# A scan, an ELU layer and a gated layer in one kernel: three reorderings in the first block

## The chip, the cores and the metric

The kernel runs on one core of a Trainium2 chip. The metric is the device time of one execution, in microseconds (us); of several runs the median counts. The engines are TensorE (PE, its weight loads apart as PEld), VectorE (DVE), ScalarE (ACT), GpSimd (POOL) and the transfer queue of SyncE (SP), which issues every DMA.

## The reference

Three steps follow each other on 3072 tokens: a chunked scan over 4 batches of 768 positions and 8 heads, and two feed-forward layers on its output.

```python
# per chunk: la = log(clip(a)), cum = cumsum(la)
L = exp(cum[i] - cum[j]) * causal
y = (C @ B.T * L) @ x + (C @ state) * exp(cum)
state = exp(sum(la)) * state + sum_j(B x exp(cum[-1] - cum[j]))
# x = y as (3072 tokens, 256)
h = x @ w_in                                   # 256 -> 2048
g = where(h > 0, h, exp(min(h, 0)) - 1)
x = g @ w_out                                  # 2048 -> 256
g = x @ w_gate; val = x @ w_val                # 256 -> 1536
out = (g * sigmoid(g) * val) @ w_out2          # 1536 -> 256
```

All weights come as 64-bit floats and must first be turned into 32-bit ones; matmuls are done in pieces of a high and a low part, to keep the accuracy.

## The kernel before

The 3072 tokens are cut into six blocks of 512. A **slot** is one pair of a block and a tile of 128 hidden units: sixteen slots a block in the first layer (96 in all), then twelve a block in the gated layer (72). The main loop runs over slots, and in each it writes out, in this order: the matmuls h of the slot (`m_a`, L489), the tasks listed under `early`, the first evacuation of h on ACT (L511), the exponential (L516) and the maximum on DVE (L517), the second matmuls c of an earlier slot (two slots back in block 0, `m_c`, L531), and then the tasks listed under `mid` and under `late`. The order written out is the order of each engine's queue: nothing reorders it later.

The scan is cut into 24 **units** of 128 tokens. Units 0 to 3, needed for block 0, come first by a hand-written list (`ORDER`). The units of block b+1 run inside the slots of block b, four of them: units 4 to 7 in block 0, at slots 0, 3, 6 and 9 (`FIRST`). From unit 8 on a unit begins every four slots, three slots earlier than a block's own count would have it (`BASE`), so unit 8 begins in slot 13 of block 0. `OFF` and `OFF1` say for each stage of a unit in which slot after its first one it stands, and in which list ("e", "m" and "l" for early, mid and late). Units from 8 on (`CUT`) have another form: their scores cb (`pe1`, L366) need operands zb and zc, split in a high part on ACT (`hi`, L294) and a low part, zb's on POOL and zc's on DVE (`lo`, L300). A unit's loads (`a_load`: abc L250 or L255, bcraw L241 or L243, ahn) are asked two units ahead. The stages that matter below are u (L388, matmuls into the accumulators y), y (L447, L454), out (xh, L470, ACT reads y) and xl (L474, DVE reads y). From unit 4 on all units share one set of accumulators.

In block 0 the weights of the first layer are still being made ready, tile by tile (f = 0 to 15; the first three ahead of the slots). Tile f takes these steps:

- `load_w1(f)`: SP asks for 512 KB into one of five areas of the buffer w2e, in turn by f modulo 5 (L127).
- `ex_w1(f)`: ACT makes e from the words with the exponents (L133). e has a single buffer.
- `dec_w1(f)`: three steps on DVE, d0 (L136) and d1 (L139) from the raw words and d2 (L143), which needs e, make the 32-bit value v.
- `pair_w1(f)`: ACT rounds v to the high part w1h (L175), and POOL subtracts, which gives the low part w1l (L179).

In slot s the kernel makes e of tile s+4 and loads tile s+7; it decodes tile s+3 and makes its pair.

Of the kernel before, what the change touches and what calls it, by code (L numbers as in the profile page):

```python
# [22 lines left out]
CUT = 8  # L23
# [15 lines left out]
OFF = dict(hi=(-1, "l"), lo=(0, "m"), scan=(0, "l"), pe1=(1, "l"), mid=(2, "m"), u=(2, "l"), state=(3, "e"), pe2=(4, "l"), out=(4, "l"), xl=(4, "l"))  # L39

OFF1 = dict(OFF, hi=(-2, "l"), lo=(-1, "m"), pe1=(0, "l"), u=(4, "l"), state=(5, "e"))
W2S = 16
FIRST = [0,3,6,9]
RAWB = 2
# [3 lines left out]
LEAD = 4  # L48
# [18 lines left out]
def ssm_mlp_glu_kernel(ctx, tc, a, bcs, xbc, w1, w2, consts, out):  # L67
# [117 lines left out]
    spare, at = {}, [0, 0]  # L185
# [450 lines left out]
    with tc.manual_schedule():  # L636
# [3 lines left out]
        nw = NW  # L640
# [25 lines left out]
        early, mid, pe, late = {}, {}, {}, {}  # L666
        late[8] = [(lambda: nc.scalar.activation(ident8, ident.unsqueeze(1).to_broadcast([128, H, Q]), AF.Copy), ())]

        def at(when, slot, fn, *args):
            when.setdefault(slot, []).append((fn, args))  # L670

        t = n0
        for b in range(NB - 1):
            n_u = BLOCKS[b + 1] // Q
            step = NF1 // n_u
            for k in range(n_u):
                s0 = b * NF1 + (FIRST[k] if b == 0 else k * step + BASE)
                off, order = (OFF, list(STAGES)) if t < CUT else (OFF1, "hi lo scan pe1 mid pe2 u out xl state".split())
                for st in order:
                    fn, (o, w) = STAGES[st], off[st]  # L680
                    at(dict(e=early, m=mid, p=pe, l=late)[w], s0 + o, fn, t)
                for x in [t + 1 + (t + 1 < CUT)] if t != CUT - 2 else []:
                    if n0 + 1 < x < NU:
                        at(late, s0 + OFF["pe1"][0], a_load_x, x)
                if t + 2 < NU:
                    at(late, s0 + OFF["pe1"][0], a_load, t + 2)
                t += 1
        for f in range(nw, NF1):
            at(mid, f - nw - 1, ex_w1, f)
            at(early, f - nw, dec_w1, f)  # L690
            at(late, f - nw, pair_w1, f)
            if f >= 4:
                at(late, max(-2, f - nw - LEAD), load_w1, f)
        last_a = (NB - 1) * NF1 - 1

        def open_a():
# [11 lines left out]

        at(late, W2S - 4, load_w2)
        for i in range(W2S, last_a):  # L710
            at(late, i, step_w2, W2K[(i - BASE) % 4], NE)
# [23 lines left out]
        for i in range(-2, len(seq) + LAG):  # L735
# [20 lines left out]
            elif i >= NF1 + LAG:  # L756
                b, f = seq[i - LAG]
# [68 lines left out]
```

## Time and profile before

| | us |
|---|---|
| median of 3 runs | 661.53 |
| lowest, highest | 660.57, 662.37 |
| the profiled execution | 662.88 |
| its span, first to last instruction | 661.1 |
| PE busy in the span | 628.7 |
| DVE busy | 386.7 |
| ACT busy | 312.0 |
| POOL busy | 315.3 |

The span is what the profile shows; the 1.78 us beside it lie before the first and after the last instruction. The mean granted clock of PE over the span was 0.997. Block 0 of the first layer runs from 36.3 us to about 100 us, the rest of the first layer and the gated layer behind it.

### The profile page before, as it was taken

To read this page: it belongs to the slowest core of one execution; us is meant where nothing else is said; L and a number is where in the kernel's file an instruction comes from. 1 tells how busy PE (TensorE), PEld (TensorE's weight loads), DVE (VectorE), ACT (ScalarE), POOL (GpSimd) and SP (SyncE) were. 2 spreads that over 40 slices of the span, in tenths; PEclk is the share of its full clock that TensorE was granted. 3 is DMA by queue.
4 is the path that set the end of the run, shared out by engine and by line. 5 is a ranking of instruction groups with operands and counts; after the bars stand their busy time and mean duration, and the time that the engine had idled before them with its cause. 6 is when DMAs were issued, how large, how long until landed. Compare 5 with 4: busy or idle time off the path is not lost.

```text
span 661.1 us, 9674 instructions
## 1 busy us (share of the span) xinstructions
PE 628.7 (95%) x3620; PEld 491.6 (74%) x3620; DVE 386.7 (58%) x580; ACT 312.0 (47%) x562; POOL 315.3 (48%) x263
## 2 busy tenths in 40 slices
PE   2589989999999999999999999999999999999997
PEld 1355556777778787777788888888888888888886
DVE  5869876887788788874564673343343343343332
ACT  2145557757666676666776442332332332332322
POOL 2535654867787677773453333333333333333332
PEclk9999989999999999999999999999999999999999
DMA  5775733544443444500310000000000000000000
GB/s 179 199 264 175 166 110 123 149 140 128 143 131 129 148 132 132 149 35 17 95 49 0 1 1 0 33 0 1 32 1 0 33 1 0 33 0 1 32 1 32
DMA packets 21646, 49.54 MB, mean 75 GB/s; under 512 B 4320, under 2 KB 6496, under 8 KB 21600
## 3 DMA queue, kind: packets, MB, share of 16 engines
q1 hardware_dynamic: 21600, 48.93, 24.1%
q8 instruction: 28, 0.46, 0.3%
q14 instruction: 18, 0.15, 0.1%
HBM read 45.68 MB, written 3.24 MB: 74 GB/s over the span
## 4 chain that ended last, share of the span: by engine, by line
PE 79%; DVE 9%; DMA 4%; issue 2%; ACT 2%; POOL 2%; SPq 1%; DVEq 0%; POOLq 0%; ACTq 0%
PE o L489 15%; PE g L489 15%; PE v L489 15%; PE h L489 15%; PE c L537 14%; DMA w2e<-in_w 2%; DMA raw<-in_w 2%; DVE E L312 2%; DVE m L517 1%; DVE v L139 1%; PE y L442 1%; PE c L531 1%; PE cb L366 1%; DVE v L136 1%; DVE v L143 1%
## 5 line engine op out<-in xcount | busy, mean ns | idle before, releaser
L495 POOL TENSOR_TENSOR gl<-m,gh 128x512 fp32r<-128x512 f32 x152 | 199.4, 1314 | 261.4 <-ACT gh L494 259.7
L609 DVE TENSOR_TENSOR m<-m,g 128x512 f32<-128x512 f32 x72 | 49.5, 688 | 169.9 <-ACT m L604 169.9
L604 ACT ACTIVATE m<-g 128x512 f32<-128x512 f32 x72 | 43.1, 598 | 191.6 <-PE g L489 191.6
L517 DVE SCALAR_TENSOR_TENSOR m<-m,h 128x512 f32<-128x512 f32 x96 | 65.5, 683 | 64.6 <-ACT m L516 64.6
L494 ACT ACTIVATE gh<-m 128x512 fp32r<-128x512 f32 x152 | 94.7, 623 | 1.6 <-DVE m L610 1.0
L511 ACT ACTIVATE m<-h 128x512 f32<-128x512 f32 x96 | 57.0, 594 | 70.8 <-PE h L489 68.5
L489 PE MATMUL h<-xh,w1h 128*128 128x512 f32 x192 | 81.7, 426 | 1.3 <-DVE xl L474 1.0
L489 PE MATMUL h<-xh,w1l 128*128 128x512 f32 x192 | 77.1, 401 | 0.0
L537 PE MATMUL c<-gh,w1h 128*128 128x512 f32 x160 | 63.5, 397 | 0.9 <-DVE x L543 0.9
L537 PE MATMUL c<-gh,w1l 128*128 128x512 f32 x160 | 63.2, 395 | 0.0
L489 PE MATMUL h<-xl,w1h 128*128 128x512 f32 x192 | 60.5, 397 | 0.0
L516 ACT ACTIVATE m<-m 128x512 f32<-128x512 f32 x96 | 59.8, 623 | 0.5
L489 PE MATMUL g<-x2h,w2h 128*128 128x512 f32 x144 | 56.9, 395 | 0.0
L489 PE MATMUL v<-x2h,w2h 128*128 128x512 f32 x144 | 56.8, 394 | 0.0
L489 PE MATMUL o<-gh,w2l 128*128 128x512 f32 x144 | 56.8, 394 | 0.0
L489 PE MATMUL o<-gl,w2h 128*128 128x512 f32 x144 | 56.8, 394 | 0.0
L489 PE MATMUL g<-x2h,w2l 128*128 128x512 f32 x144 | 56.8, 394 | 0.0
L489 PE MATMUL o<-gh,w2h 128*128 128x512 f32 x144 | 56.8, 394 | 0.0
L489 PE MATMUL v<-x2h,w2l 128*128 128x512 f32 x144 | 56.5, 392 | 0.0
L610 DVE TENSOR_TENSOR m<-m,v 128x512 f32<-128x512 f32 x72 | 49.5, 688 | 8.2 <-DVE m L609 0.9
L537 PE MATMUL c<-gl,w1h 128*128 128x512 f32 x160 | 50.3, 395 | 0.0
L489 PEld LDWEIGHTS h<-xh,w1h 128*128 128x128 f32 x192 | 36.8, 192 | 13.1 <-DVE m L517 1.8
(126 smaller groups left out, 1091.1 us busy)
## 6 DMA issues: line engine op xcount, KB each, us to landing
abc<-ac SPq DMA_DIRECT2D x16, 512.0 KB
bcraw<-in_bcs SPq DMA_DIRECT2D x32, 256.0 KB
raw<-in_w SPq DMA_DIRECT2D x15, 512.0 KB
w2e<-in_w SPq DMA_DIRECT2D x12, 512.0 KB
xb<-in_xbc SPq DMA_DIRECT2D x17, 256.0 KB
raw<-in_w SPq DMA_DIRECT2D x12, 256.0 KB
out_y<-yo SPq DMA_DIRECT2D x12, 256.0 KB
abc<-ac SPq DMA_DIRECT2D x8, 128.0 KB
```

The source lines that it names most:

```text
L136: nc.vector.tensor_scalar(halves(v)[:, :, 0], t["h16"][:, :, 1], 13, None, ALU.logical_shift_right)
L312: nc.vector.tensor_tensor_scan(u["E"].rearrange("p h q -> p (h q)"), u["abc"].rearrange("p h q -> p (h q)"), ident8.rearrange("p h q -> p ...
L489: nc.tensor.matmul(dst, lhsT=l, rhs=r, start=first and i == 0, stop=last and i == len(ops) - 1, **kw)
L494: nc.scalar.activation(hi, src, AF.Copy)
L495: lo_eng.tensor_tensor(lo, src, hi.bitcast(F32), ALU.subtract)
L511: nc.scalar.activation(m, h, AF.Relu, scale=-1.0)
L516: nc.scalar.activation(m, m, AF.Exp, scale=-1.0)
L517: nc.vector.scalar_tensor_tensor(m, m, -1.0, h, ALU.add, ALU.max)
L537: nc.tensor.matmul(cps[b][m], lhsT=w[:, m * 128:(m + 1) * 128], rhs=r, start=f == 0 and w is wh and r is gh, stop=f == NF1 - 1 and r is gl)
L604: nc.scalar.activation(m, pg, AF.Sigmoid)
L609: nc.vector.tensor_tensor(m, m, pg, ALU.mult)
L610: nc.vector.tensor_tensor(m, m, pv, ALU.mult)
```

## The change

Three things move; no instruction is added or removed. `ex_w1(f)` goes from the mid list to the late list of the same slot, where it comes after the stages of units and after `pair_w1`. `load_w1(f)`, from tile 4 on, goes from late to mid. And unit 8 gets a row of offsets of its own: its high parts, low parts and scores stand one slot later than in `OFF1`, the scores behind the other stages of the slot.

```diff
--- before.py
+++ after.py
@@ -39,6 +39,7 @@
 OFF = dict(hi=(-1, "l"), lo=(0, "m"), scan=(0, "l"), pe1=(1, "l"), mid=(2, "m"), u=(2, "l"), state=(3, "e"), pe2=(4, "l"), out=(4, "l"), xl=(4, "l"))
 
 OFF1 = dict(OFF, hi=(-2, "l"), lo=(-1, "m"), pe1=(0, "l"), u=(4, "l"), state=(5, "e"))
+OFF8 = dict(OFF1, hi=(-1, "l"), lo=(0, "m"), pe1=(1, "l"))
 W2S = 16
 FIRST = [0,3,6,9]
 RAWB = 2
@@ -676,6 +677,8 @@
             for k in range(n_u):
                 s0 = b * NF1 + (FIRST[k] if b == 0 else k * step + BASE)
                 off, order = (OFF, list(STAGES)) if t < CUT else (OFF1, "hi lo scan pe1 mid pe2 u out xl state".split())
+                if t == CUT:
+                    off, order = OFF8, "hi lo scan mid pe2 u pe1 out xl state".split()
                 for st in order:
                     fn, (o, w) = STAGES[st], off[st]
                     at(dict(e=early, m=mid, p=pe, l=late)[w], s0 + o, fn, t)
@@ -686,11 +689,11 @@
                     at(late, s0 + OFF["pe1"][0], a_load, t + 2)
                 t += 1
         for f in range(nw, NF1):
-            at(mid, f - nw - 1, ex_w1, f)
+            at(late, f - nw - 1, ex_w1, f)
             at(early, f - nw, dec_w1, f)
             at(late, f - nw, pair_w1, f)
             if f >= 4:
-                at(late, max(-2, f - nw - LEAD), load_w1, f)
+                at(mid, max(-2, f - nw - LEAD), load_w1, f)
         last_a = (NB - 1) * NF1 - 1
 
         def open_a():
```

The change adds three lines ahead of the functions, so a line of the program before has a number that is up to three lower than after: L133 is L134, L489 is L490, L366 is L367.

On ACT, slots 10 to 12 before: relu and exponential are the rows with m0, and the numbers behind w1h are the tile. e_886 is e(14), e_952 e(15), xh_647 is the output of a unit.

```order
L511 ACTIVATE m0_880<-h_869 128x512
L516 ACTIVATE m0_880<-m0_880 128x512
L133 ACTIVATE e_886<-w2e_109 128x512
L470 ACTIVATE xh_647<-y_117 128x2x2x64
L175 ACTIVATE w1h13_100<-v_876 128x512
L511 ACTIVATE m0_945<-h_934 128x512
L516 ACTIVATE m0_945<-m0_945 128x512
L133 ACTIVATE e_952<-w2e_109 128x512
L294 ACTIVATE zb_962<-bcraw_796,con_65 128x512
L294 ACTIVATE zc_964<-bcraw_796,con_65 128x512
L175 ACTIVATE w1h14_102<-v_941 128x512
L511 ACTIVATE m0_983<-h_968 128x512
```

The same stretch in the changed kernel, where e_932 is e(14) and e_962 e(15):

```order
L512 ACTIVATE m0_880<-h_869 128x512
L517 ACTIVATE m0_880<-m0_880 128x512
L471 ACTIVATE xh_646<-y_117 128x2x2x64
L176 ACTIVATE w1h13_100<-v_876 128x512
L134 ACTIVATE e_932<-w2e_109 128x512
L512 ACTIVATE m0_945<-h_934 128x512
L517 ACTIVATE m0_945<-m0_945 128x512
L176 ACTIVATE w1h14_102<-v_941 128x512
L134 ACTIVATE e_962<-w2e_109 128x512
L512 ACTIVATE m0_979<-h_964 128x512
L517 ACTIVATE m0_979<-m0_979 128x512
L295 ACTIVATE zb_985<-bcraw_795,con_65 128x512
```

xh and w1h13 now come ahead of e(14), and the two operands of unit 8, zb and zc, stand behind the exponential of slot 12 and ahead of w1h15.

On SP, before, from the loads of unit 7 (abc to ahn, with bcraw in two pieces) to the x of unit 9: the three w2e loads behind unit 7 are tiles 11, 12 and 13, the two behind unit 8 are 14 and 15.

```order
L255 DMA abc<-ac 64x512 x2
L241 DMA bcraw<-in_bcs 16x1024 x2
L276 DMA ahn<-ac 128x1x64 x2
L127 DMA w2e<-in_w 128x1024 x3
L250 DMA abc<-ac 128x1024
L243 DMA bcraw<-in_bcs 64x1x1024 x2
L271 DMA ahn<-ac 128x1x128
L127 DMA w2e<-in_w 128x1024 x2
L261 DMA xb<-in_xbc 128x512
```

And in the changed kernel:

```order
L256 DMA abc<-ac 64x512 x2
L242 DMA bcraw<-in_bcs 16x1024 x2
L277 DMA ahn<-ac 128x1x64 x2
L128 DMA w2e<-in_w 128x1024 x3
L251 DMA abc<-ac 128x1024
L244 DMA bcraw<-in_bcs 64x1x1024 x2
L272 DMA ahn<-ac 128x1x128
L128 DMA w2e<-in_w 128x1024
L262 DMA xb<-in_xbc 128x512
```

The three loads behind unit 7 are now tiles 12, 13 and 14, and behind unit 8 stands tile 15 alone. Tiles 8 and 11 have passed the loads of units 6 and 7 in the same way.

On PE, before, from the second matmuls of slot 11 to those of slot 12: y is unit 7's, cb unit 8's.

```order
L531 MATMUL c0_558<-m0_945,v_811 128x512
L531 MATMUL c1_559<-m0_945,v_811 128x512
L447 MATMUL y_117<-x2_67,sbd1_130 128x128 x2
L454 MATMUL y_117<-E_862,x2_67 32x64 x16
L366 MATMUL cb_116<-zc_964,zb_962 128x128 x8
L489 MATMUL h_1043<-xh_276,w1h14_102 128x512
L489 MATMUL h_1043<-xh_276,w1l14_103 128x512
L489 MATMUL h_1043<-xh_276,w1h14_102 128x512
L489 MATMUL h_1043<-xh_276,w1l14_103 128x512
L489 MATMUL h_1043<-xl_277,w1h14_102 128x512 x2
L531 MATMUL c0_558<-m0_983,v_846 128x512
```

In the changed kernel:

```order
L532 MATMUL c0_558<-m0_945,v_811 128x512
L532 MATMUL c1_559<-m0_945,v_811 128x512
L448 MATMUL y_117<-x2_67,sbd1_130 128x128 x2
L455 MATMUL y_117<-E_860,x2_67 32x64 x16
L490 MATMUL h_1035<-xh_276,w1h14_102 128x512
L490 MATMUL h_1035<-xh_276,w1l14_103 128x512
L490 MATMUL h_1035<-xh_276,w1h14_102 128x512
L490 MATMUL h_1035<-xh_276,w1l14_103 128x512
L490 MATMUL h_1035<-xl_277,w1h14_102 128x512 x2
L532 MATMUL c0_558<-m0_979,v_846 128x512
L532 MATMUL c1_559<-m0_979,v_846 128x512
L367 MATMUL cb_116<-zc_987,zb_985 128x128 x8
L490 MATMUL h_1065<-xh_276,w1h15_104 128x512
```

The scores cb have gone from a place ahead of the matmuls h of tile 14 to one behind the second matmuls of tile 12, ahead of h of tile 15.

## Rows read from the trace of the kernel before

**Rows 1.** The page, part 1: busy time of PE, its share, its instructions.
```profile
PE 628.7 (95%) x3620; PEld 491.6 (74%) x3620; DVE 386.7 (58%) x580; ACT 312.0 (47%) x562; POOL 315.3 (48%) x263
```

**Rows 2.** Waits of PE from 40 us on: total us, times, longest.
```profile
PE y L388 <- issue: 2.3, 1, 2.3
PE y L388 <- POOL w1l L179: 1.9, 2, 1.5
...
PE cb L366 <- POOL zb L300: 0.5, 1, 0.5
```

**Rows 3.** Timeline of PE: start, duration, instruction, idle time before it and its releaser.
```profile
58.43 0.32 PE L388 MATMUL y<-x 64*32 64x64 f32 x8 [1.47 <-POOL w1l L179]
...
70.33 0.35 PE L388 MATMUL y<-x 64*32 64x64 f32 x16 [0.42 <-POOL w1l L179]
...
73.42 0.80 PE L489 MATMUL h<-xh,w1h 128*128 128x512 f32 x1
...
84.32 0.47 PE L388 MATMUL y<-x 64*32 64x64 f32 x16 [2.29 <-issue]
...
88.81 0.79 PE L489 MATMUL h<-xh,w1h 128*128 128x512 f32 x1
...
93.93 0.66 PE L366 MATMUL cb<-zc,zb 64*128 64x128 f32 x8 [0.55 <-POOL zb L300]
...
97.35 0.80 PE L489 MATMUL h<-xh,w1h 128*128 128x512 f32 x1
```

**Rows 4.** Timeline of POOL, columns as in rows 3.
```profile
58.47 1.34 POOL L179 TENSOR_TENSOR w1l<-v,w1h 128x512 fp32r<-128x512 f32 x1 [0.45 <-ACT w1h L175]
...
92.60 1.27 POOL L300 TENSOR_TENSOR zb<-bcraw,zb 128x512 fp32r<-128x512 f32 x1
```

**Rows 5.** Timeline of DVE.
```profile
57.91 0.42 DVE L474 TENSOR_TENSOR xl<-y,xh 128x256 fp32r<-128x256 f32 x1 [0.41 <-ACT xh L470]
58.25 0.45 DVE L136 TENSOR_SCALAR v<-w2e 128x512 uint16<-128x512 uint16 x1
58.59 1.54 DVE L139 TENSOR_SCALAR v<-w2e 128x512 uint16<-128x512 uint16 x1
...
69.81 0.42 DVE L474 TENSOR_TENSOR xl<-y,xh 128x256 fp32r<-128x256 f32 x1 [0.42 <-ACT xh L470]
...
80.86 0.68 DVE L517 SCALAR_TENSOR_TENSOR m<-m,h 128x512 f32<-128x512 f32 x1
83.79 0.42 DVE L474 TENSOR_TENSOR xl<-y,xh 128x256 fp32r<-128x256 f32 x1 [2.26 <-ACT xh L470]
...
86.03 0.69 DVE L143 SCALAR_TENSOR_TENSOR v<-e,v 128x512 uint32<-128x512 uint32 x1
```

**Rows 6.** Timeline of ACT.
```profile
56.93 0.68 ACT L133 ACTIVATE e<-w2e 128x512 f32<-128x512 f32 x1 [1.72 <-DVE v L143]
57.52 0.36 ACT L470 ACTIVATE xh<-y 128x256 fp32r<-128x256 f32 x1
...
82.83 0.66 ACT L133 ACTIVATE e<-w2e 128x512 f32<-128x512 f32 x1 [3.62 <-DMA w2e<-in_w]
...
86.76 0.68 ACT L133 ACTIVATE e<-w2e 128x512 f32<-128x512 f32 x1 [1.33 <-DVE v L143]
```

**Rows 7.** The chain that ended last, 64 to 85 us: start, duration, what.
```profile
62.63 1.43 DVE v L139
...
69.45 13.30 DMA w2e<-in_w
```

**Rows 8.** Timeline of SP: when DMAs were issued, columns as in rows 3.
```profile
67.11 0.33 SPq L250 DMA_DIRECT2D abc<-ac  x1
...
69.45 0.89 SPq L127 DMA_DIRECT2D w2e<-in_w  x2
```

**Rows 9.** Stretches: busy us of each engine (instructions), PE's granted clock, DMA share, GB/s.
```profile
84.00:88.00 4.00, 3.68 (x24) 2.73 (x25) 3.96 (x7) 2.64 (x6) 1.33 (x1) 0.57 0.55 208
64.50:67.50 3.00, 3.00 (x74) 2.28 (x73) 3.00 (x7) 2.28 (x4) 1.44 (x3) 1.00 0.03 7
```

## The prediction

> **What bounds the kernel now.** The page comes first. TensorE (PE) is busy 95% of the span [rows 1], so only time in which PE stands still, or runs at half clock, can be won. The list of what PE waits for, from 40 us on, has three entries that bear on this change: u L388 2.3 us with no releaser named, u twice after POOL, 1.9 together, and cb L366 0.5 us after zb [rows 2]. These 4.7 us all lie in block 0, and the timeline of PE gives their places: 1.47 us before u(5), 0.42 before u(6), 2.29 before u(7), 0.55 before cb(8) [rows 3]. I write u(t) for unit t and e(f), d0(f), d1(f), d2(f), w1h(f), w1l(f) for tile f.
>
> What does u wait for? The releaser column says w1l, or nothing, but w1l(8) starts at 58.47 [rows 4], after u(5) began at 58.43, so that reading falls. The timeline of VectorE (DVE) gives a better one: xl ends at 57.91 + 0.42 = 58.33, at 69.81 + 0.42 = 70.23 and at 83.79 + 0.42 = 84.21 [rows 5], and the three u start 0.10, 0.10 and 0.11 us later [rows 3]. u(t+1) writes the accumulators that xl(t) has to read first. And xl waits for xh on ScalarE (ACT): DVE was idle 0.41, 0.42 and 2.26 us for it [rows 5]. On ACT, xh stands behind e: e(8) starts at 56.93 after waiting for DVE's d2, xh follows at 57.52. e(14) waits 3.62 us for a DMA, and starts at 82.83 [rows 6]. The chain that ended last says how long that DMA took: 13.30 us from 69.45 on, after a stretch in which it runs through DVE [rows 7]. The transfer queue (SP) shows why: load 14 was asked at 69.45 behind all loads of unit 8, the first of them at 67.11 [rows 8].
>
> So PE's losses in block 0 are: a late transfer, behind it an ACT queue in which xh is stuck, then xl, then u. The 2.29 us have a second price. From 84 to 88 us PE was granted 0.57 of its clock, that is, most of the stretch at 1.2 GHz and not at 2.4 [rows 9]; from 64.5 to 67.5, with no wait in it, 1.00.
>
> **The change part by part.** It adds and removes no instruction; it reorders.
>
> *Load 14 ahead of unit 8's loads.* Its buffer is that of tile 9, free when d1(9) ends, 62.63 + 1.43 = 64.06 [rows 7]; unit 8's first load is held until 67.11 [rows 8] because its own buffer is not free, so load 14 now leaves about 3 us before it. The transfer engines are idle then: share 0.03, 7 GB/s from 64.5 to 67.5 [rows 9]. e(14) wants the data at about 81 us, with some 15 us of slack; the 3.62 us wait goes. Loads 8 and 11 pass the loads of units 6 and 7 likewise. e(8) waited for DVE and not for its transfer [rows 6], so I cost these two at nothing: the cover is that the unit loads which they pass are read some six slots later; without it each would cost the time of one load. Load 15 keeps its place behind unit 8's loads, is now first after them, and inherits the landing of load 14, 82.75 us (69.45 + 13.30) at the latest. That is what is late next, and a rival below.
>
> *What the missing wait gives.* xl(6) then follows L517(10), which ends at 80.86 + 0.68 = 81.54, and no longer starts at 83.79 [rows 5]: 2.25 us earlier, and ends near 81.96. u(7) stood ready behind c(9), free from 84.32 - 2.29 = 82.03 [rows 3]. So the whole **2.29 us** goes. The clock: from u(7) to h(13) took 88.81 - 84.32 = 4.49 us; the same work, u(6), h, c, at full clock took 73.42 - 70.33 = 3.09 [rows 3]. **1.40 us** go if no wait of this size is left.
>
> *Conversions e behind pairs and evacuations.* xh no longer stands behind e, and e no longer ahead of w1h. xh(4) needs only y, long finished, so xl(4) follows L517 at once: DVE's 0.41 and 0.42 us before xl(4) and xl(5) go, which moves u(5) and u(6) by at least 0.41 and 0.83. DVE has further gain: w1h, and with it w1l on POOL, starts 0.59 us earlier (57.52 - 56.93, the place that e gave up [rows 6]). d1(8) took 1.54 us while w1l ran, d0(8) 0.45 just ahead of it [rows 4, 5]; d1 ends some 0.3 us after w1l does (58.59 + 1.54 = 60.13 against 58.47 + 1.34 = 59.81), so an earlier w1l lets DVE go on earlier. Bounds: below 0.83, above both PE waits whole, 1.47 + 0.42 = 1.89. I take **1.2**, nearer the lower, because in the slot of a unit's scan POOL has that unit's products (L342, L350) ahead of w1l. The price of e coming later: e ends about two ACT operations, 1.2 us, after d2 of the tile before, and the d2 that needs it starts later than that (d0 and d1 lie between, 0.45 us each at least, and L517, 0.68). Hidden; without d0 and d1 between it would cost 0.6 us a slot.
>
> *Unit 8's scores a slot later.* cb(8) no longer stands before h(14), where PE waited 0.55 us, but behind c(12). Same eight matmuls. PE reaches it at 97.35 - 2.29 - 1.40 - 0.55 - 0.66 (its own old run) = 92.45, less the 1.2. zb, last on POOL, now follows w1l(15), which follows d2(15). d2(14) ended at 86.03 + 0.69 = 86.72, and xl comes 2.25 earlier: 84.5. d2(15) follows by an estimated 3.6 (the 2.93 from xl to the end of d2(14), plus an L517), 88.1; w1h 0.6, w1l 1.34, zb 1.27 [rows 4]: 91.3, less the 1.2. It is there 1.1 us early, and **0.55 us** go. If not, the bound is the 1.27 us of one more POOL operation ahead.
>
> The **sum**: 2.29 + 1.40 + 0.55 + 1.2 = 5.44 us, between 5.07 and 6.13 by the bounds of the third term. The profiled execution took 662.88 (span 661.1), so 657.4 for a like one. The median of the runs is 661.53, 1.35 lower: 656.1. Behind block 0 PE has no wait on any of the moved things, so what is won there stays.
>
> **The rivals.**
> *The stall moves one tile on.* Load 15 lands late, and e(15) holds ACT as e(14) did. It stands behind w1h(14): d2(14) at 84.5 less 1.2, plus 0.6, so e(15) wants its data from 83.9 us on. It lands by 82.75 if it takes load 14's place, and in the trace it was there by 86.76, where e(15) waited for DVE only [rows 6]. At worst PE feels all of it: a stall as long as the old one brings the 2.29 and the 1.40 back, the rest stays: 5.44 - 3.69 = 1.75 won, 659.8. I give it 0.10.
>
> *Slots 12 to 15 are too tight.* All work of unit 8 falls on POOL and DVE in those slots, with no stall left to hide it: cb(8) waits for zb, or h(16) for L517 behind unit 8's scan E. One POOL operation each, 1.3, and as much of the clock again: 2.5 of the 5.44 lost, 658.6. 0.14.
>
> *DVE and POOL get in each other's way more: slower.* Where d0 or d1 runs into w1l it takes 1.54 and not 0.45 us, 1.09 more [rows 5]. w1l now starts 0.59 earlier, under d0, and a POOL operation behind it (sbd, the next w1l, the unit's products) may then catch d1 too. One more hit in eight of the twelve slots with decoding is 8.7 us of DVE, which the chain says is the path there [rows 7]: 661.53 - 5.44 + 8.7 = 664.8. It decides from five slots on. Against it: POOL's total is unchanged, and DVE gets its turn at the end of each w1l. 0.06.
> The Trainium skill, page "SBUF — State Buffer", section "Who interferes with whom", has a rule by which this rival would come true: DVE in a two-port mode and POOL share a port pair as an exclusive lock, held for the whole instruction by whoever issues first, so that an earlier w1l can win the lock ahead of d0. The trace agrees as to the lock: the blocked 1.54 us end only after w1l has; which of the two wins in the new order no row here shows.
>
> *It does not do what it says.* Load 14 or an issue ahead of it is held by something that the trace doesn't show, and lands no earlier than now. Then e(14) still waits, though xh has gone ahead of it, and the decoding of tile 14 is late for h(14) instead: no change, about 661. 0.06.
>
> **How the numbers follow.** The forecast, 656.1, has 0.64, its own range 655.0 to 657.6 (the bounds of the third term, and the 0.9 us by which runs stray from their median). With the tight slots that is 0.78, with the moved stall 0.88, so the range is 654.8 to 660.0. What a measurement of this kernel can tell from no change is about 0.3%, 2 us. Faster: 0.64 + 0.14 + half of the moved stall 0.05 = 0.83; the same: 0.05 + 0.06 = 0.11; slower 0.06.
>
> **What would show it.** No wait of ACT's e for a DMA in block 0; load 14 asked between 62 and 65 us; xh on ACT ahead of w1h and right behind the exponential; u(5), u(6), u(7) with under 0.5 us of idle PE before each; PE's granted clock at 1.00 from 40 us to the end; h(15), at 97.35 before, near 91.9 (the same work lies ahead of it). It would be wrong if e(15) waits for a DMA, if d0 and d1 both take over 1 us in most slots, or if cb(8) stands after zb with over 1 us of idle PE.

## The result

The changed kernel takes 656.22 us (median; 656.04 to 656.39), the kernel before 661.86 (660.57 to 662.37). That is 5.64 us won, where 5.44 were forecast. The ratio with its 95% interval is 0.9906 (0.9885 to 0.9927); the two medians alone give 0.9915.

| | before | after |
|---|---|---|
| median, us | 661.86 | 656.22 |
| profiled execution, us | 662.88 | 656.09 |
| its span, us | 661.1 | 654.3 |
| PE's mean granted clock | 0.997 | 1.000 |

The spans of the two profiled executions differ by 6.8 us, more than the medians. A part of that lies ahead of anything that the change touches: the first h of block 0 starts at 36.31 us before and at 35.23 after. In the profiles of the experiments below, whose kernels are alike up to there, it starts anywhere from 34.92 to 36.34, so this part is chance.

First the waits of PE after the change, from 36 us to the end, with the total in us, how many there were, and the longest; they answer to [rows 2].

```profile
PE h L490 <- DVE xl L475: 1.0, 1, 1.0
PE c L538 <- DVE x L544: 0.9, 3, 0.5
PE y L389 <- issue: 0.5, 2, 0.4
```

The 2.3, 1.9 and 0.5 us of [rows 2] have become 0.5 in all. The entry of 1.0 stands at the first h of block 0, the 0.9 at the ends of blocks, and the change touches neither; both are there before as well. The timeline of PE, with idle time in brackets, gives the places; it answers to [rows 3].

```profile
56.48 0.32 PE L389 MATMUL y<-x 64*32 64x64 f32 x8 [0.36 <-issue]
...
67.89 0.34 PE L389 MATMUL y<-x 64*32 64x64 f32 x16
...
79.35 0.35 PE L389 MATMUL y<-x 64*32 64x64 f32 x16 [0.19 <-issue]
...
82.66 0.57 PE L490 MATMUL h<-xh,w1h 128*128 128x512 f32 x1
...
90.16 0.66 PE L367 MATMUL cb<-zc,zb 64*128 64x128 f32 x8
90.75 0.50 PE L490 MATMUL h<-xh,w1h 128*128 128x512 f32 x1
```

u(5) waits 0.36 us where it waited 1.47, u(6) not at all, u(7) 0.19 in place of 2.29, and cb(8) not at all. From u(7) to h(13) it takes 82.66 - 79.35 = 3.31 us in place of 4.49. ACT and DVE show why (rows 5 and 6 of before, in one slot).

```profile
76.52 0.37 ACT L471 ACTIVATE xh<-y 128x256 fp32r<-128x256 f32 x1
78.35 0.63 ACT L176 ACTIVATE w1h<-v 128x512 fp32r<-128x512 f32 x1 [1.47 <-DVE v L144]
78.89 0.66 ACT L134 ACTIVATE e<-w2e 128x512 f32<-128x512 f32 x1
...
82.58 0.66 ACT L134 ACTIVATE e<-w2e 128x512 f32<-128x512 f32 x1
```

```profile
78.24 0.68 DVE L518 SCALAR_TENSOR_TENSOR m<-m,h 128x512 f32<-128x512 f32 x1
78.83 0.42 DVE L475 TENSOR_TENSOR xl<-y,xh 128x256 fp32r<-128x256 f32 x1
79.17 0.61 DVE L137 TENSOR_SCALAR v<-w2e 128x512 uint16<-128x512 uint16 x1
79.67 1.54 DVE L140 TENSOR_SCALAR v<-w2e 128x512 uint16<-128x512 uint16 x1
```

xh(6) runs at 76.52, right behind the exponential and 1.8 us ahead of w1h; e(14) at 78.89 and e(15) at 82.58 wait for nothing; xl(6) follows L518 without a gap. d1 still takes 1.54 us while a w1l runs on POOL. The transfer queue issues three w2e loads ahead of unit 8's loads, with load 14 the last of them, in a stretch that ends at 57.95 + 4.81 = 62.76, and unit 8's first load at 65.11; before, load 14 was asked behind unit 8 [rows 8].

```profile
57.95 4.81 SPq L128 DMA_DIRECT2D w2e<-in_w  x3
65.11 0.33 SPq L251 DMA_DIRECT2D abc<-ac  x1
...
67.47 0.79 SPq L128 DMA_DIRECT2D w2e<-in_w  x1
```

PE's granted clock, in the stretch of [rows 9], is 1.00 now, where it was 0.57:

```profile
84.00:88.00 4.00, 4.00 (x47) 2.61 (x46) 2.65 (x5) 3.49 (x7) 2.71 (x4) 1.00 0.28 100
```

### The profile page after: what moved, and what is told of

It is laid out like the page before. It is cut to its first block, busy times and chain, and to the rows that moved or that the text cites. A ratio compares the mean times of both kernels' runs of the same rounds, so it can differ in the third digit from the quotient of the medians.

```text
span 654.3 us, 9659 instructions
## 1 busy us (share of the span) xinstructions
PE 627.9 (96%) x3620; PEld 490.6 (75%) x3620; DVE 387.8 (59%) x580; ACT 312.3 (48%) x562; POOL 314.9 (48%) x263
## 4 chain that ended last, share of the span: by engine, by line
PE 87%; DVE 5%; DMA 2%; issue 2%; POOL 1%; ACT 1%; SPq 1%; POOLq 0%; DVEq 0%; ACTq 0%
PE h L490 18%; PE o L490 15%; PE g L490 15%; PE v L490 15%; PE c L538 14%; PE c L532 4%; DMA raw<-in_w 2%; DVE E L313 1%; PE y L443 1%; PE cb L367 1%; DVE m L518 1%; PE y L439 1%; POOL xb L337 1%; DVE w2e L137 1%; DMA w2e<-in_xbc 1%
## 5 line engine op out<-in xcount | busy, mean ns | idle before, releaser
L518 DVE SCALAR_TENSOR_TENSOR m<-m,h 128x512 f32<-128x512 f32 x96 | 65.5, 683 | 62.8 <-ACT m L517 62.8
L490 PE MATMUL h<-xh,w1h 128*128 128x512 f32 x192 | 80.5, 419 | 1.0 <-DVE xl L475 1.0
L490 PE MATMUL h<-xh,w1l 128*128 128x512 f32 x192 | 76.8, 400 | 0.0
L517 ACT ACTIVATE m<-m 128x512 f32<-128x512 f32 x96 | 59.9, 624 | 0.5
L490 PE MATMUL h<-xl,w1h 128*128 128x512 f32 x192 | 60.1, 394 | 0.0
L490 PE MATMUL g<-x2h,w2h 128*128 128x512 f32 x144 | 56.8, 395 | 0.0
L490 PE MATMUL v<-x2h,w2h 128*128 128x512 f32 x144 | 56.7, 394 | 0.0
L490 PE MATMUL o<-gh,w2l 128*128 128x512 f32 x144 | 56.7, 394 | 0.0
L490 PE MATMUL o<-gl,w2h 128*128 128x512 f32 x144 | 56.7, 394 | 0.0
L490 PE MATMUL g<-x2h,w2l 128*128 128x512 f32 x144 | 56.7, 394 | 0.0
L490 PE MATMUL o<-gh,w2h 128*128 128x512 f32 x144 | 56.7, 394 | 0.0
L490 PE MATMUL v<-x2h,w2l 128*128 128x512 f32 x144 | 56.4, 392 | 0.0
L490 PEld LDWEIGHTS h<-xh,w1h 128*128 128x128 f32 x192 | 36.5, 190 | 13.4 <-DVE m L518 2.9
```

Source lines behind the costliest of these rows:

```text
L490: nc.tensor.matmul(dst, lhsT=l, rhs=r, start=first and i == 0, stop=last and i == len(ops) - 1, **kw)
L517: nc.scalar.activation(m, m, AF.Exp, scale=-1.0)
L518: nc.vector.scalar_tensor_tensor(m, m, -1.0, h, ALU.add, ALU.max)
```

## The experiments

Each group of four was run beside the kernel before, on the same chip: its medians are 661.62 us for the first four, 662.07 for the next four, 661.96 for the last four. **Won** is against those. The ratio is not that of the two medians, and can differ from it by about 0.1%.

| what | median, us | won | ratio (95%) |
|---|---|---|---|
| loads alone | 661.21 | 0.41 | 0.9988 (0.9969 to 1.0008) |
| load 14 alone | 661.34 | 0.28 | 0.9989 (0.9974 to 1.0004) |
| conversions alone | 657.81 | 3.81 | 0.9945 (0.9929 to 0.9961) |
| unit 8 alone | 659.26 | 2.36 | 0.9973 (0.9951 to 0.9995) |
| all but unit 8 | 657.21 | 4.86 | 0.9926 (0.9913 to 0.9938) |
| all but the loads | 656.67 | 5.40 | 0.9918 (0.9904 to 0.9931) |
| all but the conversions | 658.48 | 3.59 | 0.9943 (0.9929 to 0.9956) |
| all, e between xh and the pair | 658.22 | 3.85 | 0.9941 (0.9929 to 0.9954) |
| all, w1l on DVE | 658.85 | 3.11 | 0.9942 (0.9921 to 0.9962) |
| the same, e between xh and the pair | 660.46 | 1.50 | 0.9969 (0.9956 to 0.9983) |
| all, block ends reordered | 655.15 | 6.81 | 0.9885 (0.9863 to 0.9908) |
| all, w1l on DVE, block ends reordered | 657.18 | 4.78 | 0.9917 (0.9895 to 0.9939) |

### Each part alone

The theory is the sum of the prediction: each term belongs to one part of the change. The rival is that a wait needs two causes at once, so that parts do not add up. The loads:

```diff
-                at(late, max(-2, f - nw - LEAD), load_w1, f)
+                at(mid, max(-2, f - nw - LEAD), load_w1, f)
```

Expected: 

> The loads alone are moved (load_w1 from late to mid); conversions and unit 8 as before. Theory of the sum: the late transfer is the cause of the 2.29 us wait and of the lost clock, so both go here and nothing else does: 3.7 us won, about 658.2 against 661.9, u(7) with under 0.5 us of idle PE, u(5) still with about 1.4 and cb(8) with about 0.5. Rival (the transfer was hidden anyway and ACT's order is the cause): no change, u(7) keeps about 2 us of idle PE.

Only 0.41 us were won, which cannot be told from nothing. But the rival does not hold either: u(7) no longer waits 2 us, as the waits of PE show.

```profile
PE y L388 <- POOL w1l L179: 2.1, 3, 1.2
PE y L447 <- POOL sbd L413: 1.3, 1, 1.3
...
PE cb L366 <- POOL zb L300: 0.5, 1, 0.5
```

u(7) waits 0.47 us, as forecast, but y(7), which waited for nothing before, now waits 1.25 for POOL. cb(8) waits 0.54, as it did before (0.55). ACT and then POOL in that place:

```profile
83.96 0.68 ACT L133 ACTIVATE e<-w2e 128x512 f32<-128x512 f32 x1 [1.35 <-DVE v L143]
84.55 0.71 ACT L294 ACTIVATE zb<-bcraw,con 128x512 fp32r<-128x512 f32 x1
85.16 0.71 ACT L294 ACTIVATE zc<-bcraw,con 128x512 fp32r<-128x512 f32 x1
85.78 0.62 ACT L175 ACTIVATE w1h<-v 128x512 fp32r<-128x512 f32 x1
```

```profile
86.47 1.82 POOL L179 TENSOR_TENSOR w1l<-v,w1h 128x512 fp32r<-128x512 f32 x1 [3.58 <-ACT w1h L175]
88.25 1.60 POOL L413 TENSOR_TENSOR sbd<-sc,con 128x256 f32<-128x256 f32 x2
```

On ACT zb and zc of unit 8 stand between e(15) and w1h(14). POOL idles 3.58 us until w1h(14) is there, and sbd of unit 7, which y(7) needs, comes behind that w1l. In the kernel before, the stall ahead of u(7) had hidden this, because PE came to y(7) late enough. The stall had moved to the next thing in line. And in this execution the clock fell after the new waits, as the second row shows (PE's granted clock is the column of 1.00 and 0.57):

```profile
84.00:92.00 8.00, 6.20 (x58) 3.68 (x57) 5.86 (x13) 5.51 (x10) 5.53 (x5) 1.00 0.39 107
92.00:96.00 4.00, 4.00 (x9) 2.45 (x9) 3.10 (x3) 1.23 (x2) 3.03 (x3) 0.57 0.04 16
```

With load 14 alone:

```diff
-                at(late, max(-2, f - nw - LEAD), load_w1, f)
+                at(mid if f == 14 else late, max(-2, f - nw - LEAD), load_w1, f)
```

Expected: 

> Of the loads only that of tile 14 is moved ahead of unit 8's; the rest as before. Theory of the sum: loads 8 and 11 are worth nothing, so this comes out as the run with all loads moved, about 658.2. Rival: the other two moved loads carry part of the gain or cost some, then the two differ by more than 0.5 us.

661.34 against 661.21: loads 8 and 11 are worth nothing that these runs can tell, as was said; the size was wrong as above.

The conversions:

```diff
-            at(mid, f - nw - 1, ex_w1, f)
+            at(late, f - nw - 1, ex_w1, f)
```

Expected: 

> The conversions e alone are moved behind the stages of units and behind the pairs; loads and unit 8 as before. Theory of the sum: e(14) still waits for its transfer, here about 3 us, and holds the evacuations of slot 11 behind it, so the 2.29 us and the lost clock stay for the larger part and only the third term comes: 1.2 to 1.9 us won, about 660.4. Rival (the stall needs two things at once, a late transfer and an xh that stands behind it): xh(6) has gone ahead, PE has two slots of h in hand, and the stall goes without any load being moved: 4.9 us or more won, about 657, with e(14) still waiting for a DMA while PE waits under 0.5 us before u(7).

The rival holds in its mechanism, though not in its size: 3.81 us are won with no load moved. e(14) waits for its transfer still, but only 0.63 us, and u(7) waits 0.22. With a wait that short this run alone does not show that a late transfer is harmless; the run without the loads, below, had one of 2.27 us. The one wait of PE in block 0 over 0.4 us is that of cb(8), which PE now reaches early:

```profile
PE cb L366 <- DVE zc L300: 1.4, 1, 1.4
...
PE y L388 <- issue: 0.6, 2, 0.4
```

Unit 8's offsets, without the other parts:

```diff
+OFF8 = dict(OFF1, hi=(-1, "l"), lo=(0, "m"), pe1=(1, "l"))
...
+                if t == CUT:
+                    off, order = OFF8, "hi lo scan mid pe2 u pe1 out xl state".split()
```

Expected: 

> Unit 8's offsets alone are changed; loads and conversions as before. Theory of the sum: the 0.55 us before cb(8) go and nothing else does, about 661.3, with the 2.29 us before u(7) in place. Rival: cb(8) waits in its new place as well, or the moved operands only shift the wait: 661.9 or slower.

Neither: 2.36 us were won, by an interval that leaves 0.3 to 3.2. cb(8) waits no more, and w1h(14) is no longer behind zb and zc, which the sum had given no price. u(7) waits 1.15 us and not 2.29, since e(14) waits less for its transfer:

```profile
80.31 0.66 ACT L134 ACTIVATE e<-w2e 128x512 f32<-128x512 f32 x1 [2.47 <-DMA w2e<-in_w]
```

The order of issue is that of the kernel before, but the load took 12.15 us from its issue, at 68.08, and not 13.30. So 1.14 us of what was won in this execution come from an earlier landing, and nothing shows that unit 8's offsets had a part in that.

### Each part left out

The same three edits, each taken back alone in the changed kernel:

```diff
-OFF8 = dict(OFF1, hi=(-1, "l"), lo=(0, "m"), pe1=(1, "l"))
...
-                if t == CUT:
-                    off, order = OFF8, "hi lo scan mid pe2 u pe1 out xl state".split()
```

```diff
-                at(mid, max(-2, f - nw - LEAD), load_w1, f)
+                at(late, max(-2, f - nw - LEAD), load_w1, f)
```

```diff
-            at(late, f - nw - 1, ex_w1, f)
+            at(mid, f - nw - 1, ex_w1, f)
```

Expected, without unit 8's offsets: 

> The change without its third part: loads and conversions moved, unit 8 as before. Theory now (the waits of slots 11 to 13 are linked: unit 8's operands zb and zc stand on ACT ahead of the pair of tile 14 and hold w1l(14), the sbd of unit 7 and cb(8) behind them): PE waits 1 to 1.5 us before cb(8), and the time comes out as with the conversions alone, about 657.7, 1.5 above the changed kernel. Rival, the sum of the prediction: 0.55 above the changed kernel, 656.8.

657.21, between the two theories: PE waits 0.96 us before cb(8), for zc on DVE.

Expected, without the loads: 

> The change without its loads: conversions and unit 8 moved, load 14 still behind unit 8's loads. Theory now (the late transfer costs PE something only while xh stands behind e): e(14) waits about 0.6 us for its transfer, PE waits under 0.5 us before u(7), 656.3 to 656.8. Rival, the late transfer as a cause of its own: u(7) or h(13) waits again for more than 1 us and the time is 658 or more.

656.67, as the theory of linked waits had it. A row of ACT and one of PE:

```profile
81.30 0.69 ACT L134 ACTIVATE e<-w2e 128x512 f32<-128x512 f32 x1 [2.27 <-DMA w2e<-in_w]
```

```profile
79.40 0.35 PE L389 MATMUL y<-x 64*32 64x64 f32 x16 [0.24 <-issue]
...
83.92 0.50 PE L490 MATMUL h<-xh,w1h 128*128 128x512 f32 x1 [0.85 <-DVE m L518]
```

e(14) waits 2.27 us for its transfer, more than the 0.6 expected, and yet u(7) waits 0.24 only. The late e holds up the relu and the exponential of the next slot on ACT and so the maximum L518 on DVE, and PE feels it as 0.85 us before the h that follows. So in this execution, the slowest of the four, most of a late transfer is taken up by the slots between.

Expected, without the conversions: 

> The change without its conversions: loads and unit 8 moved, e still ahead of xh and of the pair. Theory now: the waits before u(5), u(6), u(7) stay at about 1.2, 0.4 and 0.5 us and nothing else waits in block 0; 1.6 us more than the changed kernel's 0.55, 657.8 to 658.2. Rival (the order on ACT is what matters, loads and unit 8 are not): as before, 661.5.

658.48, a little over that; the three waits before u(5), u(6) and u(7) are 1.17, 0.43 and 0.47 us.

### What the place of e is worth

In the changed kernel the conversion e goes ahead of the pair w1h and w1l again, but stays behind xh:

```diff
         for f in range(nw, NF1):
             at(late, f - nw - 1, ex_w1, f)
+        for f in range(nw, NF1):
             at(early, f - nw, dec_w1, f)
             at(late, f - nw, pair_w1, f)
```

Expected: 

> The change, with the conversion e put between xh and the pair instead of behind the pair: xh goes early as in the changed kernel, w1h and w1l start 0.6 us later, as before. It splits the third term. Theory of the prediction (xl after L518 gives 0.83 us, an earlier w1l the rest): 0.4 to 1 us above the changed kernel, 656.6 to 657.2. Rival (the place of xh is all): as the changed kernel within 0.2 us.

658.22 is 2.0 above the changed kernel, more than either theory had, and only 0.26 below the kernel without the conversions. xh is early in both; only w1h, and with it w1l, comes 0.6 us later. Decoding on DVE from 40 to 82 us, grouped by line (count, total, mean ns), with e between xh and the pair, and then in the changed kernel:

```profile
L140 DVE TENSOR_SCALAR v<-w2e 128x512 uint16<-128x512 uint16 x11 | 11.0, 1004 | 0.0
L137 DVE TENSOR_SCALAR v<-w2e 128x512 uint16<-128x512 uint16 x11 | 8.4, 765 | 0.0
L144 DVE SCALAR_TENSOR_TENSOR v<-e,v 128x512 uint32<-128x512 uint32 x10 | 8.1, 809 | 1.0
```

```profile
L140 DVE TENSOR_SCALAR v<-w2e 128x512 uint16<-128x512 uint16 x11 | 11.5, 1044 | 0.0
...
L137 DVE TENSOR_SCALAR v<-w2e 128x512 uint16<-128x512 uint16 x11 | 7.9, 718 | 0.0
L144 DVE SCALAR_TENSOR_TENSOR v<-e,v 128x512 uint32<-128x512 uint32 x11 | 7.6, 692 | 1.1
```

A tile costs 1004 + 765 + 809 = 2578 ns of DVE in the one and 1044 + 718 + 692 = 2454 in the other, 0.12 us a tile or 1.4 us over eleven. It is d2 and d0 that take longer when w1l comes later.

Is it POOL that stretches them? Two kernels have w1l of tiles 3 to 15 on DVE:

```diff
-        nc.gpsimd.tensor_tensor(lo, w1s.pop(f)[0], hi.bitcast(F32), ALU.subtract)
+        (nc.vector if f >= 3 else nc.gpsimd).tensor_tensor(lo, w1s.pop(f)[0], hi.bitcast(F32), ALU.subtract)
```

Expected: 

> The changed kernel, with the low part w1l of tiles 3 to 15 subtracted on DVE instead of POOL. Theory (DVE's d0 and d1 are stretched by w1l on POOL, not by anything of their own): with w1l gone from POOL most d1 take 0.45 us instead of 1.54, DVE gains about 1.1 us and pays 0.6 us a slot, u(5) and u(7) wait under 0.2 us; PE is the bound now, so only 0.3 to 0.6 us are won, 655.7. Rival (the stretch has another cause): d1 stays at 1.5 us, DVE has 0.6 us more work a slot, 660 or more.

```profile
L180 DVE TENSOR_TENSOR w1l<-v,w1h 128x512 fp32r<-128x512 f32 x11 | 8.2, 744 | 0.1
...
L144 DVE SCALAR_TENSOR_TENSOR v<-e,v 128x512 uint32<-128x512 uint32 x10 | 6.9, 692 | 1.0
L137 DVE TENSOR_SCALAR v<-w2e 128x512 uint16<-128x512 uint16 x11 | 6.6, 598 | 0.0
L140 DVE TENSOR_SCALAR v<-w2e 128x512 uint16<-128x512 uint16 x10 | 5.9, 586 | 0.0
```

The mechanism holds: with w1l gone from POOL d1 falls from 1044 to 586 ns and d0 from 718 to 598. The forecast of a gain does not: w1l costs DVE 744 ns a tile and gives back 458 + 120, so DVE has more to do, u(5) waits 1.19 us, and 2.6 us are lost against the changed kernel.

Expected: 

> As the run with e ahead of the pair, with w1l of tiles 3 to 15 on DVE as well. It tells why the place of e was worth 2 us there. Theory (through the lock of DVE and POOL alone: a later w1l stretches d0 and d1 further): without w1l on POOL the place of e is worth nothing, the time is that of the changed kernel with w1l on DVE within 0.4 us, 655.7 to 656.3. Rival (the later w1h itself is late for something, the weights of h or ACT's queue): it stays 1 us or more above that run, 657 to 658.

660.46, 1.61 above the other, so the rival holds here. The decoding itself no longer depends on the place of e:

```profile
L144 DVE SCALAR_TENSOR_TENSOR v<-e,v 128x512 uint32<-128x512 uint32 x10 | 6.9, 692 | 0.3
L137 DVE TENSOR_SCALAR v<-w2e 128x512 uint16<-128x512 uint16 x10 | 6.1, 606 | 0.0
L140 DVE TENSOR_SCALAR v<-w2e 128x512 uint16<-128x512 uint16 x10 | 5.8, 580 | 0.0
```

The three steps take 692 + 606 + 580 = 1878 ns a tile, and 692 + 598 + 586 = 1876 with e behind the pair. So the 1.4 us above come by w1l on POOL. But the times do not separate what they were meant to: with w1l on DVE a later w1h makes DVE itself idle, 1.7 us in four waits of w1l for w1h. What makes up the 2.0 us of the place of e beyond the 1.4 stays open.

### A version that beats both

The 0.9 us of waits at the ends of blocks can go too: there the maximum on DVE is written behind the copy of the accumulators.

```diff
     def m_e1b(b, f, part=None):
...
+            ends = i == NF1 - 1 + LAG0 or (i > NF1 + LAG and i - LAG < n1 and seq[i - LAG][1] == NF1 - 1)
             if 0 <= i < n1:
-                m_e1b(*seq[i])
+                m_e1b(*seq[i], 0 if ends else None)     # 0: the exponential alone
...
+            if ends and i < n1:
+                m_e1b(*seq[i], 1)                       # 1: the maximum, behind m_end
```

Expected: 

> The changed kernel, and at each block's end the DVE copy of the accumulators (L544) ahead of the maximum L518 of that slot, for which it waited. PE waits for that copy 0.9 us in three places in the trace. Theory: these 0.9 us go, 655.3 to 655.6. Rival: the maximum, now later, makes h wait instead: no change, 656.2.

655.15 (654.51 to 655.81), 1.07 below the changed kernel, and the runs of the two do not overlap. The waits of PE, where the 0.9 us are gone and a 0.2 stands in their place:

```profile
PE h L490 <- DVE xl L475: 1.0, 1, 1.0
PE y L389 <- issue: 0.6, 2, 0.4
PE h L490 <- DVE m L520: 0.2, 1, 0.2
```

Expected, with w1l on DVE as well: 

> The changed kernel with w1l on DVE and with the copy at a block's end ahead of the maximum. If PE's remaining waits are the bound, the two add up: 654.9 to 655.3. If either only shifts a wait, it is no better than the better one of the two.

657.18: 1.67 better than w1l on DVE alone, but no better than the reordered block ends alone. w1l on DVE is a loss with them too.

## Why the prediction came out, and where it was wrong

The sum was right, 5.44 against 5.64, and so were the waits that would go: 2.29 - 0.19, 0.55, and 1.47 - 0.36 + 0.42 make 4.18 us, where its three terms for waits have 4.04. Which part of the change makes them go was not right, and that the sum fits the medians so well is in part luck, as the term for the clock shows.

**Load 14 and the 3.69 us.** The prediction's step was: with load 14 ahead of unit 8's loads the wait of e(14) goes, and with it the whole 2.29 us before u(7) and 1.40 of clock. The loads alone won 0.41 us, and left out they cost 656.67 - 656.22 = 0.45 (or 5.64 - 5.40 = 0.24, each against the kernel before run beside it). The wait before u(7) did shrink to 0.47, but 1.25 us rose two slots later ahead of y(7), where w1h(14) stood behind zb and zc. Conversely u(7) waits 0.24 us in the run without the loads, with a transfer 2.27 us late. So the stall of PE before u(7) needs a late transfer and an xh behind it; either one removed is enough. What then shows is unit 8's place on ACT. The prediction also counted "some 15 us of slack" for load 14, which is about the whole time from asking to use; with a transfer of 13.30 us, 81 - 64.06 - 13.30 = 3.6 were left.

**Unit 8: 0.55 us.** As the last part it is worth 5.64 - 4.86 = 0.78 (or 657.21 - 656.22 = 0.99), alone 2.36, of which 1.14 came by an earlier landing in the profiled execution. Only the wait before cb(8) was counted; moving zb and zc also clears the way of w1h(14), w1l(14), sbd and y(7). In the run with the loads alone PE waits 1.25 us before y(7), and in the runs with unit 8 moved not at all. PE reaches cb(8) at 90.16, or 91.24 in the time of before (1.08 later, by the start of block 0), where 91.25 was forecast. zb was to be there 1.1 us early and is there 90.16 - 88.06 - 1.27 = 0.83 early. But zc on DVE, for which the prediction had no term, comes last, only 0.28 us early, and it is what cb(8) waits for in the two runs that move the conversions but not unit 8:

```profile
88.06 1.27 POOL L301 TENSOR_TENSOR zb<-bcraw,zb 128x512 fp32r<-128x512 f32 x1
```

```profile
88.51 1.37 DVE L301 TENSOR_TENSOR zc<-bcraw,zc 128x512 fp32r<-128x512 f32 x1
```

**The conversions: 1.2 us.** Mis-sized: 5.64 - 3.59 = 2.05 us when left out (or 658.48 - 656.22 = 2.26). The bounds, 0.83 to 1.89, were right as to the two waits, of which 1.47 - 0.36 + 0.42 = 1.53 went. A further 0.28 is in u(7), which without the conversions waits 0.47 us and with them 0.19; the rest was not traced. The prediction took a value near the lower end and gave the earlier w1l little. With e ahead of the pair 2.0 us are lost, so without the earlier w1l the early xh is worth next to nothing.

**The clock: 1.40 us.** It was read from one execution in which the clock fell, and taken whole from a median of executions of which only some had a fall. Of the 32 executions of the kernel before that go with the first four experiments, 18 had a mean granted clock of 0.999 or 1.000 and a median of 661.17 us, 14 had 0.994 to 0.997 and 663.27. With the next four, 7 of 9 had 0.996 or 0.997, and with the last four 10 of 17 had 0.994 to 0.997. Against the 18 the changed kernel is 4.95 us faster, with no fall to win back. As an estimate from these numbers, the clock's term was 1.40 - (5.64 - 4.95) = 0.71 too large for the medians, and the terms for waits, 4.04 together, were 0.91 too small: two errors that cancel. Of the 4.95 us, the profiles show 4.18 in the waits of the sum and 0.26 more before an h of slot 3, which waited for a maximum (`PE h L489 <- DVE m L517: 0.3, 1, 0.3` in the list of before); the rest was not traced.

**The rivals.** The stall did not move to e(15), which waits for nothing. The slots 12 to 15 are not too tight: h(15) starts at 90.75, or 91.83 in the time of before, where 91.9 was forecast. DVE and POOL get in each other's way as much as before, in this view of the kernel before from 40 to 82 us:

```profile
L139 DVE TENSOR_SCALAR v<-w2e 128x512 uint16<-128x512 uint16 x10 | 9.2, 920 | 0.0
L143 DVE SCALAR_TENSOR_TENSOR v<-e,v 128x512 uint32<-128x512 uint32 x10 | 9.0, 901 | 0.9
...
L136 DVE TENSOR_SCALAR v<-w2e 128x512 uint16<-128x512 uint16 x10 | 6.6, 660 | 0.0
```

d0, d1 and d2 took 660 + 920 + 901 = 2481 ns a tile and take 2454 now. The hits have moved: d2 is at the 692 ns that it takes with w1l off POOL, and d0 and d1 take longer. The Trainium skill, page "SBUF — State Buffer", section "Who interferes with whom", says that an instruction of DVE in a two-port mode and one of POOL exclude each other on a shared port pair for their whole length. The trace agrees: d1 takes 1.54 us beside w1l and 586 ns in the mean without it on POOL. That did not make the new order slower.

That the moved loads are worth little holds for these landings. With load 14 behind unit 8's loads e(14) waited 3.62, 2.47, 2.27 and 0.63 us in four kernels; what sets the landing was not tried.

Two slips of the prediction change nothing. The w1l that starts at 58.47 is that of tile 7, not 8, since w1h(7) follows e(8) on ACT as w1h13 follows e(14); it still starts after u(5) began. And the forecast's own range, 655.0 to 657.6, is not what its two named parts give: 661.53 - 6.13 - 0.9 = 654.5 to 661.53 - 5.07 + 0.9 = 657.4.

## What to carry to other kernels

A wait at the end of a long chain can have two causes, and then either one removed makes it vanish. Price each part by leaving it out as well as by doing it alone: here the parts alone add up to 6.6 us and left out to 3.1 (3.7 from the medians as they are), for a change of 5.6, though each of these figures is uncertain by about 1 us. When a stall is removed, look at what it hid: the next engine in line (here ACT, with two operands of a later unit ahead of the pair) takes its place at once. And read a term for the clock from several executions before it is subtracted from a median.

## What the runs showed of the hardware

The clock fell in some executions and not in others of the same kernel. It fell in 14 of 32, 7 of 9 and 10 of 17 of the kernel before, in 5 of 12 with the loads alone, 5 of 12 with load 14 alone, 2 of 12 with the conversions alone and 3 of 9 with unit 8 alone; in none of the 4 of the changed kernel and in none of the 48 of the other eight experiments. Such an execution of the kernel before takes about 2 us more (663.27 against 661.17), with unit 8 alone 3.65 (662.66 against 659.01). The trace of the kernel before shows 1.40 us of lost clock; whether the waits are longer too in such executions is not known, since one execution of each kernel was profiled. What went before the fall was 2.29 us of idle PE in the one profile [rows 3, 9], and 1.25 and 0.54 us within three us in the other. Waits of PE as such do not tell it: with w1l on DVE and e between xh and the pair PE stood still for 0.97, 1.44, 0.40, 0.95 and 0.95 us in block 0 of the profiled execution, and none of the 12 had a fall.

A load of 512 KB took 12.15 to 13.80 us from issue to landing when it was asked behind one unit's loads on the same queue (13.30 in the kernel before, 12.16 with the conversions alone, 12.15 with unit 8 alone, 13.80 without the loads).
